# One dP tile in sixteen moved from VectorE to ScalarE and GpSimd in an attention backward

## The chip, the cores and the metric

The kernel runs on one core of one Trainium2 chip. The metric is the device time of one execution in microseconds: 2561.26 us, the median of three runs (2560.2 to 2564.32). A core has five engines that matter here: PE (TensorE, matrix products into PSUM), DVE (VectorE), ACT (ScalarE), POOL (GpSimd) and SP (SyncE, which issues DMAs). Each runs its own queue in order, and they wait for one another by semaphores.

## The reference, cut to what matters

The kernel computes the output of one transformer block and the gradients of all its inputs, for 2048 tokens, width 512, 32 heads of 16 and a feed-forward width of 1792.

```python
def _A_ref(x, wqkv, wo):
    H = 32
    Dh = D // H
    qkv = (lambda x, *d: x.transpose(*d))((x @ wqkv).reshape(B, S, 3, H, Dh), 2, 0, 3, 1, 4)
    q, k, v = (qkv[0], qkv[1], qkv[2])
    scale = Dh ** (-0.5)
    scores = jnp.einsum('bhqd,bhkd->bhqk', q, k) * scale
    p = _softmax(scores, axis=-1)
    o = jnp.einsum('bhqk,bhkd->bhqd', p, v)
    return (lambda x, *d: x.transpose(*d))(o, 0, 2, 1, 3).reshape(B, S, D) @ wo
...
h = _layernorm(x, axis=-1) * (1 + ca) + sa
x = x + ga * _A_ref(h, A_wqkv, A_wo)
h = _layernorm(x, axis=-1) * (1 + cb) + sb
x = x + gb * _B_ref(h, B_w1, B_b1, B_w2, B_b2)
...
_out, _vjp = jax.vjp(_f, A_x, A_wqkv, A_wo, B_w1, B_b1, B_w2, B_b2, c, w_mod)
_grads = _vjp(grad_out)
```

What matters here is the gradient through the softmax. With S the scores, P = exp(S) (its normalization is folded into the operands beforehand), and dO the gradient of the heads' output, the kernel forms dP = dO V^T minus a row term (two extra rows of the operand carry it), dS = P * dP, and then dQ = dS K, dK = dS^T Q, dV = P^T dO. P and dS are never kept: they are made tile by tile from Q, K, V and dO.

## The kernel before

The forward pass takes the first 1130 us or so, with the feed-forward part and its gradients around it. Then comes `attn_bwd`, the stage that the change touches, and after it `phase6`, the gradients of the projections.

**Loops.** `attn_bwd` runs over `g` (8 sets of four heads), `jp` (2 pairs of heads in a set), `c` (4 column blocks of 512 keys), `ib0` (4 groups of `G` = 4 row blocks) and `i` (a row block of 128 queries). One (g, jp, c, ib) is a *unit*; it has two tiles of 128x512, one for each head `a` of the pair. There are 1024 units, 256 groups, 2048 tiles.

**One iteration `i`** (lines 1546 to 1569) does, for its own unit, two score matmuls (L1555, into one of three PSUM buffers `st`) and two exps on ScalarE (L1559, into `pu`, bf16, six buffers). Between a score matmul and its exp stands `dP(last, a)` for the unit *before*: a matmul into one of three PSUM buffers `dp` (L1494) and a VectorE multiply by `pu` into `ds` (L1496). The score matmul uses one half of PE's rows and the dP matmul the other, so the two run side by side. After the pair `dS(last)` puts the unit on the list `pend`; at the group's last unit it issues, on SP, the crossbar DMA transpose of the group's dS (L1504) into `dsT`.

**The lists.** At odd `i` `kv_two` takes the two oldest units of `pend` and accumulates dK and dV on PE (L1448, eight matmuls for the two units, reading `ds` and `pu`). At `i` = 3 these two are the last unit of the group before and unit 0 of the present one. At even `i` two units of `pendq` give dQ on PE (L1470, 16 matmuls of 128x16 for the two units, reading `dsT`); by then their transpose was issued nearly two groups earlier, and the group that it belongs to is three back.

**The transposes.** A group's dS is 32 blocks of 128x128 (four units, two heads, four blocks). `turn_ds`, called at `i` = 2, turns the first four (unit 0, head 0) on PE through a PSUM buffer `st` (L1513), and ScalarE copies them into `dsT[:, 0:4]` (L1514). The DMA transpose turns the other 28.

**Order.** PE, SP and GpSimd follow the order in which the program was written; VectorE and ScalarE are ordered by the framework and in the trace they follow it too. GpSimd's queue in this stage holds, once for each load, a tiny copy `tick` (L1543) that reads one element of the group before's dS, so that loads keep pace with the stage, and the load's issue (L1544). The loads are for the next pair or set of heads.

**Buffers.** `ds` has three buffers, one for each group, `dsT` four. `self.junk6` is a 128x512 f32 tile used for results that nobody reads in `phase6`; `self.csq` is one of the same size for column sums after this stage.

Of the kernel before, what the change touches and what calls it, by code (L numbers as in the profile page):

```python
# [12 lines left out]
ALU = mybir.AluOpType  # L13
# [6 lines left out]
P = 128  # L20
# [85 lines left out]
class K:  # L106
# [1315 lines left out]
    def attn_bwd(self):  # L1422
# [7 lines left out]
        tc, nc = self.tc, self.nc  # L1430
        S, D, H, NQ, ST, SC = self.S, self.D, self.H, self.NQ, self.ST, self.SC
        G = 4
# [20 lines left out]
        def turn(g, jp, kvT, s0):  # L1453

            h0 = 4 * g + 2 * jp
            n = ST // 2
            tp = stp.tile([P, n, P], BF16, name="st")
            for st in range(n):
                nc.tensor.transpose(tp[:, st, :], kvT[:, (s0 + st) * P:(s0 + st + 1) * P], self.ident[:])
            v = tp[:].rearrange("p s (t a e) -> p t s a e", t=2, a=2)  # L1460
            for t, dst in enumerate((self.dk_t, self.dv_t)):
                d = dst[:, s0:s0 + n, h0 * DH:(h0 + 2) * DH].rearrange("p s (a d) -> p s a d", a=2)
                nc.scalar.copy(d, v[:, t, :, :, 0:DH])

        def dq(u, heads):
            (T, g, jp, c, ib, i, dsT) = u
            for a in heads:
                col = (2 * jp + a) * DH
                for sub in range(4):
                    nc.tensor.matmul(accq[:, ib, a, :], lhsT=dsT[:, (i * 2 + a) * 4 + sub, :],  # L1470
                                     rhs=T["K"][:, 4 * c + sub, col:col + DH],
                                     start=(c == 0 and ib == 0 and a == 0 and sub == 0), stop=False,
                                     skip_group_check=True)
            if c == SC - 1 and ib == ST - 1 and 1 in heads:
                h0 = 4 * g + 2 * jp
                d = self.dq_t[:, :, h0 * DH:(h0 + 2) * DH].rearrange("p s (a d) -> p s a d", a=2)
                nc.vector.tensor_scalar(d, accq[:], self.scale, None, ALU.mult)

        def kv_two(n=2):
            for u in pend[2 - n:2]:  # L1480
                kv(u)
            (T, g, jp, c, ib, kvT, pu, ds) = pend[1]
            del pend[:2]
            if c % 2 and ib == ST - 1 and (g, jp) == (NQ - 1, 1):
                turnq.append((g, jp, kvT, 4 * (c - 1)))
            elif c == SC - 1 and ib == ST - 1:
                turnq.extend((g, jp, kvT, s0) for s0 in (0, ST // 2))

        def dP(u, a):

            (T, g, jp, c, ib, kvT, pu, dsg, i, grp) = u
            rd = slice(64 - 64 * jp, 128 - 64 * jp)
            dp = dpp.tile([P, 512], F32, name="dp")
            nc.tensor.matmul(dp[:], lhsT=T["dOT"][rd, ib * P:(ib + 1) * P],  # L1494
                             rhs=masked["VT"][2 * jp + a][rd, 512 * c:512 * (c + 1)], start=True, stop=True)
            nc.vector.tensor_tensor(dsg[:, i, a], dp[:], pu[:, a, :], ALU.mult)  # L1496

        def dS(u):

            (T, g, jp, c, ib, kvT, pu, dsg, i, grp) = u  # L1500
            pend.append((T, g, jp, c, ib, kvT, pu, dsg[:, i]))
            if i == G - 1:
                dsT = grp[0]
                nc.sync.dma_start_transpose(dsT[:, 4:, :], dsg[:].rearrange("p i a k -> p (i a k)")[:, 512:])  # L1504
                for i in range(G):
                    pendq.append((T, g, jp, c, ib - G + 1 + i, i, dsT))

        def turn_ds(dsg, grp):

            dsT = dtp.tile([P, 8 * G, P], BF16, name="dsT")  # L1510
            tp = stp.tile([P, 4, P], BF16, name="st")
            for b in range(4):
                nc.tensor.transpose(tp[:, b, :], dsg[:, 0, 0, b * P:(b + 1) * P], self.ident[:])  # L1513
            nc.scalar.copy(dsT[:, 0:4, :], tp[:])  # L1514
            grp.append(dsT)

        tick = self.tick
        T = self.T0
        turnq, last = [], None
        for g in range(NQ):  # L1520
            for jp in range(2):
                if jp == 0:
                    if g + 1 < NQ:
                        Tn, later = self.load_group(g + 1)
                    else:
                        Tn, later = None, self.wq_pieces(1) + self.load_wmt()
                    cut = len(later) // 2 if Tn else len(later)
                    pieces = self.pair_pieces(g, 1) + later[:cut]
                    later = later[cut:]
                elif g + 1 < NQ:  # L1530
                    pieces = self.pair_pieces(g + 1, 0) + later
                else:
                    pieces = [(self.xhat1_6[:, st, :], self.xhat1_d.rearrange("(st p) d -> p st d", p=P)[:, st, :])
                              for st in range(ST)]
                kvT = kvp.tile([P, S], BF16, name="kvT")
                total = len(pieces)
                for c in range(SC):
                    c0 = 512 * c
                    for ib0 in range(0, ST, G):
                        m = c * (ST // G) + ib0 // G  # L1540
                        while pieces and (total - len(pieces)) * SC * ST <= m * G * total:
                            if last:
                                nc.gpsimd.tensor_copy(tick[:], last[7][0:1, 0, 0, 0:1])  # L1543
                            nc.gpsimd.dma_start(*pieces.pop(0))  # L1544
                        dsg, grp = self.dsp.tile([P, G, 2, 512], BF16, name="ds"), []
                        for i in range(G):
                            ib = ib0 + i
                            q = slice(ib * P, (ib + 1) * P)
                            if turnq and i == 2:
                                turn(*turnq.pop(0))  # L1550
                            pu = self.pup.tile([P, 2, 512], BF16, name="pu")
                            for a in range(2):
                                stt = stp.tile([P, 512], F32, name="st")
                                rs = slice(64 * jp, 64 * jp + 64)
                                nc.tensor.matmul(stt[:], lhsT=T["QT"][rs, q], rhs=masked["KT"][2 * jp + a][rs, c0:c0 + 512],  # L1555
                                                 start=True, stop=True)
                                if last:
                                    dP(last, a)
                                nc.scalar.activation(pu[:, a, :], stt[:], ACT.Exp, scale=self.scale)  # L1559
                            if last:  # L1560
                                dS(last)
                            last = (T, g, jp, c, ib, kvT, pu, dsg, i, grp)
                            if i % 2 == 1 and len(pend) >= 4:
                                kv_two()
                            elif i % 2 == 0 and len(pendq) > 2 * G:
                                for _ in range(4 if len(pendq) > 3 * G else 2):
                                    dq(pendq.pop(0), [0, 1])
                            if i == 2:
                                turn_ds(dsg, grp)
            T = Tn  # L1570
        with tc.manual_schedule(engines=ALL):
            for t in (2, 0):
# [338 lines left out]
```

The softmax here doesn't subtract the row's maximum and nothing guards it: scores larger than these inputs give would overflow.

## Time and profile before

| what | value |
|---|---|
| median of the runs | 2561.26 us (2561.26, 2564.32, 2560.2) |
| span of the profiled execution, first to last instruction | 2562.0 us |
| granted PE clock, mean over the span | 0.994 |
| PE busy over the span | 2483.2 us (97%) |
| ScalarE busy | 2314.2 us (90%) |
| VectorE busy | 1767.4 us (69%) |
| GpSimd busy | 569.5 us (22%) |
| first and last DMA transpose of dS (L1504) | 1185.6 and 2440.0 us |
| from one group to the next, undisturbed | 4.78 us |

The profile is of one execution; its own time is not listed apart from its span. The span lies inside the spread of the runs. Lines of the profile name the source line, the engine, the operation, and `out<-in` by the program's tile names; a figure in the last column is idle time of the engine before such instructions, with what ended it. In a row of the timeline instructions of one kind that follow one another are merged (`x21`), with the start of the first and the length from there to the end of the last. Matmuls overlap: the length of one says less than the distance between starts.

### The profile page before, as it was taken

What the parts mean: (1) busy time and instruction counts of PE and PEld (TensorE: products, weight loads), DVE (VectorE), ACT (ScalarE), POOL (GpSimd) and SP (SyncE); (2) the same over time, 40 slices, a digit from 0 to 9 for tenths busy, and PEclk for the clock granted to TensorE, in tenths of its full rate; (3) what the DMA queues carried; (4) which work ended last, traced back from release to release, by engine and by line L of the source; (5) the groups of instructions that cost most, each with busy time, mean ns of one, the idle gap of its engine ahead of it and who ended that gap; (6) DMA issues with size and microseconds to landing.
All of it is one profiled execution on the core that took longest, in us unless ns stands there. A gap on an engine that the chain in (4) does not pass through costs nothing.

```text
span 2562.0 us, 77852 instructions
## 1 busy us (share of the span) xinstructions
PE 2483.2 (97%) x31239; PEld 1227.4 (48%) x31239; DVE 1767.4 (69%) x3651; ACT 2314.2 (90%) x3757; POOL 569.5 (22%) x1137
## 2 busy tenths in 40 slices
PE   8999899999999999899999999999999999999998
PEld 4555555555555554663444444444444444444443
DVE  6222323323322344667999999999999999999957
ACT  7999999999999996436999999999999999999935
POOL 3554521320221131353011111111111111111223
PEclk9999999999999999999999999999999999999999
DMA  4588742450351153799999999999999999999997
GB/s 165 118 180 196 173 95 83 100 113 22 112 128 49 39 143 113 154 190 211 205 205 202 199 200 201 203 204 200 197 199 198 208 201 197 201 201 229 213 202 191
DMA packets 1193040, 425.37 MB, mean 166 GB/s; under 512 B 1138004, under 2 KB 1161686, under 8 KB 1192678
## 3 DMA queue, kind: packets, MB, share of 16 engines
q1 hardware_dynamic: 1153542, 319.25, 64.2%
q0 software_dynamic: 37056, 100.11, 13.1%
q8 instruction: 244, 4.00, 0.6%
q10 hardware_dynamic: 2080, 1.05, 0.1%
q14 instruction: 118, 0.97, 0.1%
HBM read 73.73 MB, written 62.40 MB: 53 GB/s over the span
## 4 chain that ended last, share of the span: by engine, by line
PE 67%; ACT 20%; DMA 5%; issue 4%; POOL 2%; DVE 1%; SPq 1%; POOLq 0%; DVEq 0%; ACTq 0%
PE st L1555 20%; ACT pu L391 16%; PE acckv L1448 11%; PE accq L1470 8%; PE st L388 7%; PE accbank L322 3%; PE dp L1494 3%; ACT pu L1559 2%; PE st L1513 2%; PE dps L1047 2%; PE pps L1234 2%; PE dp L1604 1%; PE st L1699 1%; DMA dsT<-ds 1%; DMA ev_tm<-ev_fm 1%
## 5 line engine op out<-in xcount | busy, mean ns | idle before, releaser
L1496 DVE TENSOR_TENSOR ds<-dp,pu 128x512 bf16<-128x512 f32 x2048 | 1236.2, 679 | 13.1 <-PE dp L1494 10.2
L1559 ACT ACTIVATE pu<-st 128x512 bf16<-128x512 f32 x2048 | 1073.7, 612 | 46.4 <-PE dp L1494 22.5
L391 ACT ACTIVATE pu<-st 128x1024 bf16<-128x1024 f32 x992 | 912.1, 1077 | 4.6 <-PE st L388 4.4
L388 PE MATMUL st<-QTm,KTq 128*128 128x512 bf16 x1984 | 588.6, 377 | 19.5 <-ACT pu L391 6.0
L322 PEld LDWEIGHTS <-pu 128*128 128x128 bf16 x8192 | 347.5, 96 | 236.1 <-issue 3.1
L322 PE MATMUL accbank<-Vaug,pu 128*128 128x17 bf16 x8192 | 357.7, 171 | 1.2 <-ACT Vaug L522 0.9
L1494 PE MATMUL dp<-m,q 64*128 64x512 bf16 x1024 | 345.7, 382 | 1.1 <-DVE g2w L1053 0.7
L1494 PE MATMUL dp<-m,dOTg 64*128 64x512 bf16 x1024 | 344.6, 381 | 0.1
L1470 PEld LDWEIGHTS <-dsT 128*128 128x128 bf16 x8192 | 239.5, 96 | 213.8 <-issue 209.7
L1555 PE MATMUL st<-m,q 64*128 64x512 bf16 x1024 | 319.5, 382 | 9.2 <-ACT pu L1559 7.5
L1555 PE MATMUL st<-m,QTg 64*128 64x512 bf16 x1024 | 318.9, 381 | 9.5 <-ACT pu L1559 7.8
L388 PEld LDWEIGHTS <-KTq 128*128 128x128 bf16 x1984 | 188.3, 96 | 176.9 <-issue 125.5
L1543 POOL COPY tick<-ds 1x1 bf16<-1x1 bf16 x223 | 39.6, 178 | 1005.4 <-DVE ds L1496 1005.4
L1448 PE MATMUL acckv<-ds,q 128*16 128x512 bf16 x1024 | 154.0, 381 | 0.0
L1448 PE MATMUL acckv<-pu,dOg 128*16 128x512 bf16 x1024 | 154.0, 381 | 0.0
L1448 PE MATMUL acckv<-ds,Qg 128*16 128x512 bf16 x1024 | 154.0, 381 | 0.0
L1448 PE MATMUL acckv<-pu,q 128*16 128x512 bf16 x1024 | 154.0, 381 | 0.0
L1514 ACT COPY dsT<-st 128x512 bf16<-128x512 bf16 x256 | 152.4, 595 | 1.0 <-PE st L1513 1.0
L1470 PE MATMUL accq<-Kg,dsT 128*128 128x16 bf16 x4096 | 143.3, 170 | 3.4 <-DMA dsT<-ds 3.4
L1470 PE MATMUL accq<-q,dsT 128*128 128x16 bf16 x4096 | 143.6, 170 | 0.4 <-DMA dsT<-ds 0.3
L302 POOL DMA_DIRECT2D QTm<-QTq_d x124 | 63.3, 512 | 341.3 <-PE st L388 320.2
L329 DVE RECIPROCAL rl<-accbank 128x4 f32<-128x4 f32 x128 | 22.9, 179 | 162.6 <-PE accbank L322 162.5
(379 smaller groups left out, 2864.8 us busy)
## 6 DMA issues: line engine op xcount, KB each, us to landing
KTq<-KTq_d POOLq DMA_DIRECT2D x24, 512.0 KB, 3.9
duT_d<-auT POOLq DMA_DIRECT2D x3, 1792.0 KB, 7.8
aT_d<-rT POOLq DMA_DIRECT2D x3, 1792.0 KB, 11.1
KTq_d<-KTq SPq DMA_DIRECT2D x32, 128.0 KB, 2.0
QTq_d<-ev_fm SPq DMA_DIRECT2D x32, 128.0 KB, 3.9
VTq_d<-vT POOLq DMA_DIRECT2D x4, 1024.0 KB, 6.8
dsT<-ds SPq DMA_TRANSPOSE x256, 6.7
dx<-dx_d SPq DMA_DIRECT2D x16, 256.0 KB, 4.4
```

Source lines behind the costliest of these rows:

```text
L302: nc.gpsimd.dma_start(QTm[j][32 * j:32 * j + 32, :], self.QTq_d[g, 32 * j:32 * j + 32, 512 * qc:512 * (qc + 1)])
L322: nc.tensor.matmul(acc[:, a, sub, :], lhsT=pu[:, a, sub * P:(sub + 1) * P], rhs=Vaug[:, kb, h, :], start=(kb == 0 and a == 0 and sub == 0) ...
L388: nc.tensor.matmul(stt[:, a, :], lhsT=KT[:, kb * P:(kb + 1) * P], rhs=QTm[2 * jp + a][:], start=True, stop=True)
L391: nc.scalar.activation(pu[:], stt[:], ACT.Exp, scale=self.scale)
L1047: nc.tensor.matmul(pt[:], lhsT=a[st], rhs=g_tm[:, st, :], start=(st == 0), stop=(st == ST - 1))
L1448: nc.tensor.matmul(acckv[r:r + DH, :], lhsT=T[n][:, ib, col:col + DH], rhs=src[:, a, :], start=(ib == 0), stop=(ib == ST - 1))
L1470: nc.tensor.matmul(accq[:, ib, a, :], lhsT=dsT[:, (i * 2 + a) * 4 + sub, :], rhs=T["K"][:, 4 * c + sub, col:col + DH], start=(c == 0 and i ...
L1494: nc.tensor.matmul(dp[:], lhsT=T["dOT"][rd, ib * P:(ib + 1) * P], rhs=masked["VT"][2 * jp + a][rd, 512 * c:512 * (c + 1)], start=True, sto ...
L1496: nc.vector.tensor_tensor(dsg[:, i, a], dp[:], pu[:, a, :], ALU.mult)
L1514: nc.scalar.copy(dsT[:, 0:4, :], tp[:])
L1555: nc.tensor.matmul(stt[:], lhsT=T["QT"][rs, q], rhs=masked["KT"][2 * jp + a][rs, c0:c0 + 512], start=True, stop=True)
L1559: nc.scalar.activation(pu[:, a, :], stt[:], ACT.Exp, scale=self.scale)
```

## The change

In every second group (`off(c, ib)`: the second and fourth of the four groups of a column block), one of the eight dP tiles, unit 0 and head 1, isn't multiplied by VectorE. `dP` returns the PSUM tile instead; after the exp that follows, ScalarE copies it to one of two f32 scratch tiles (`junk6` and `csq` in turn) and GpSimd multiplies the copy by P into the same place of `ds`. In the same groups `turn_ds` takes a `dsT` buffer but does no PE transposes and no ScalarE copy, and the DMA transpose turns all 32 blocks.

```diff
             nc.tensor.matmul(dp[:], lhsT=T["dOT"][rd, ib * P:(ib + 1) * P],
                              rhs=masked["VT"][2 * jp + a][rd, 512 * c:512 * (c + 1)], start=True, stop=True)
+            if a == 1 and i == 0 and off(c, ib):
+                return dp
             nc.vector.tensor_tensor(dsg[:, i, a], dp[:], pu[:, a, :], ALU.mult)
+
+        def off(c, ib):
+            return (c * SC + ib // G) % 2 == 1
+
+        def dP_pool(u, dp):
+            (T, g, jp, c, ib, kvT, pu, dsg, i, grp) = u
+            f = (self.junk6, self.csq)[(c * SC + ib // G) // 2 % 2]
+            nc.scalar.copy(f[:], dp[:])
+            nc.gpsimd.tensor_tensor(dsg[:, i, 1], f[:], pu[:, 1, :], ALU.mult)
...
             if i == G - 1:
-                dsT = grp[0]
-                nc.sync.dma_start_transpose(dsT[:, 4:, :], dsg[:].rearrange("p i a k -> p (i a k)")[:, 512:])
+                dsT, n = grp
+                nc.sync.dma_start_transpose(dsT[:, n:, :], dsg[:].rearrange("p i a k -> p (i a k)")[:, n * P:])
...
-        def turn_ds(dsg, grp):
+        def turn_ds(dsg, grp, skip):
 
             dsT = dtp.tile([P, 8 * G, P], BF16, name="dsT")
+            grp.extend((dsT, 0 if skip else 4))
+            if skip:
+                return
             tp = stp.tile([P, 4, P], BF16, name="st")
             for b in range(4):
                 nc.tensor.transpose(tp[:, b, :], dsg[:, 0, 0, b * P:(b + 1) * P], self.ident[:])
             nc.scalar.copy(dsT[:, 0:4, :], tp[:])
-            grp.append(dsT)
...
-                                if last:
-                                    dP(last, a)
+                                held = dP(last, a) if last else None
                                 nc.scalar.activation(pu[:, a, :], stt[:], ACT.Exp, scale=self.scale)
+                                if held is not None:
+                                    dP_pool(last, held)
...
                             if i == 2:
-                                turn_ds(dsg, grp)
+                                turn_ds(dsg, grp, off(c, ib))
```

## The prediction

> **What bounds the kernel now.** The change touches only the backward attention stage (about 1179 to 2443 us), so I read the page for the engines, then windows of the stage, the timeline of one group of four units, the chain, and last the landings of the crossbar transposes. A group is one pass of the `ib0` loop: four units, eight dP tiles, one transpose of dS by SP. There are 256. I write (u,a) for the tile of unit u of a group and head a.
>
> From the page, then two windows of 4.78 us, one group each (columns: engine busy us and count, PE clock, DMA share, GB/s):
>
> ```profile
> PE 2483.2 (97%) x31239; PEld 1227.4 (48%) x31239; DVE 1767.4 (69%) x3651; ACT 2314.2 (90%) x3757; POOL 569.5 (22%) x1137
> ...
> L1496 DVE TENSOR_TENSOR ds<-dp,pu 128x512 bf16<-128x512 f32 x2048 | 1236.2, 679 | 13.1 <-PE dp L1494 10.2
> ...
> L1514 ACT COPY dsT<-st 128x512 bf16<-128x512 bf16 x256 | 152.4, 595 | 1.0 <-PE st L1513 1.0
> ...
> 1697.00:1701.78 4.78, 4.78 (x77) 2.08 (x74) 4.78 (x9) 4.77 (x11) 0.63 (x3) 1.00 0.90 208
> 1701.78:1706.57 4.78, 4.78 (x73) 2.00 (x71) 4.78 (x9) 4.63 (x10) 0.69 (x3) 1.00 1.00 209
> ```
>
> PE, VectorE and ScalarE all look full, at full clock, and GpSimd is idle. Which one sets the pace is decided by who waits. VectorE's row has 13 us of idle time in 1236. The timeline (start, length, engine, line):
>
> ```profile
> 1699.69 12.63 DVE L1496 TENSOR_TENSOR ds<-dp,pu 128x512 bf16<-128x512 f32 x21
> 1702.64 3.07 ACT L1559 ACTIVATE pu<-st 128x512 bf16<-128x512 f32 x6
> 1705.87 1.08 ACT L1559 ACTIVATE pu<-st 128x512 bf16<-128x512 f32 x2 [0.16 <-PE dp L1494]
> 1706.94 0.59 ACT L1514 COPY dsT<-st 128x512 bf16<-128x512 bf16 x1
> ...
> 1704.81 0.17 PE dp L1494
> 1706.05 0.12 PE dp L1494
> ```
>
> Twenty-one VectorE multiplies without a gap take 12.63 us, so one starts every (12.63 - 0.68)/20 = 0.598 us, and eight are 4.78 us, exactly the group's period (the PE transposes start at 1701.74, 1706.52, 1711.31). The last two lines are of the chain: PE's second dP matmul of a pair starts late, by 0.17, 0.12 and (at 1703.73) 0.05 us, because its PSUM buffer, one of three, is still with VectorE. So VectorE is the bound; PE could do a group in 4.78 - 0.34 = 4.44 us. ScalarE starts an activation every (3.07 - 0.61)/5 = 0.49 us; nine are 4.4 us.
>
> **The change, part by part.** It acts in every second group ("odd", 128 of them).
>
> VectorE loses one multiply in an odd group: at most 0.598 us, over 128 groups 76.5 us. That is the ceiling of the gain.
>
> PE loses four transposes in an odd group: the chain has them as "PE st L1513 x4", 0.24 us. PE could do an odd group in 4.20.
>
> ScalarE loses the copy of the transposed block (595 ns) and gains a copy of 128x512 f32 out of PSUM; the same form elsewhere takes 572 to 598 (L1762, L1071, L1621). Net nothing. But it sits elsewhere: after the second exp of the iteration i=1, where the trace starts the next exp at 1705.87. The exps of i=2 come 0.2 us later (1706.07); the VectorE multiply that needs the first starts at about 1707.1, and it is ready at 1706.66, so 0.4 us cover this. The copy waits for a dP matmul that is over at 1704.98, long before its turn.
>
> GpSimd gains 128 multiplies of 128x512. None of this mixed form is in the trace; the nearest are L1147 (bf16 by f32 into bf16) at 1163 ns and L1054 (all f32) at 1283. I take L1147, whose types are the same in the other order, and keep 1.28 as the other end. GpSimd's own queue: a tick and a load issue stand behind the multiply and go from 1705.88 to about 1707.5; the loads are for a later pass of 16 groups, which covers 1.6 us. Would it slow VectorE? Where L1054 ran at 1180.28 for 1.28 us, three ds multiplies beside it took
>
> ```profile
> 1180.28 1.28 POOL L1054 TENSOR_TENSOR dgb_acc<-dgb_acc,g2w 128x512 f32<-128x512 f32 x1
> 1180.61 1.89 DVE L1496 TENSOR_TENSOR ds<-dp,pu 128x512 bf16<-128x512 f32 x3
> ```
>
> which is (1.89 - 0.68)/2 = 0.605 apart: no more than 0.01 us. Zero, then. In contrast the VectorE cast L1158 has a median of 424 ns and a longest of 1379, among GpSimd's L1112. The Trainium skill ("SBUF — State Buffer", on who interferes with whom) says that GpSimd and some VectorE instructions lock each other out of a shared port for a whole instruction, but not one with a single SBUF input in a one-port mode, as ds has; were the lock to hold here, 128 x 1.2 us would be lost and the sum would be some +77 us.
>
> Now the order. I follow one odd group with the trace's times for what comes before. VectorE starts dS tile (0,0) at 1705.07 and could start (1,0), now next in line, at 1705.67; but that dP matmul starts on PE at 1705.45, after the kv matmuls, and ends at 1705.83, so VectorE starts at 1705.90: 0.23 us of the 0.598 are lost to PE's order. Then it runs (1,1) at 1706.50, (2,0) at 1707.10, (2,1) at 1707.70, and is free for (3,0) at 1708.30.
>
> PE meanwhile has the one new wait. The second kv unit of iteration i=3 reads the GpSimd tile. In the trace its matmuls start at 1707.59; without the transposes at 1707.35. The ScalarE copy starts at 1705.60 (0.48 after the exp at 1705.13) and ends at 1706.19. GpSimd starts 0.13 later (what the tick takes after its VectorE write, 1705.75 to 1705.88), ends at 1706.32 + 1.16 = 1707.48, and PE goes on at about 1707.56: a stall of 0.21, which eats most of the 0.24 of the transposes. Queued behind it: 0.32 of kv, then the pair with dP (3,0), over 0.385 later, and VectorE 0.075 after: 1707.56 + 0.78 = 1708.34 against 1708.30. So 0.04 more lost; with 1.28 us on GpSimd, 0.16. VectorE's gain per odd group is 0.598 - 0.23 - 0.04 = 0.33 us (0.21 at the slow end; 0.37 with no stall). In the even group after it PE starts 0.33 behind its old lead and has its 0.34 of buffer waits to make that up, so VectorE stays the bound there. 128 x 0.33 = 42 us.
>
> The Trainium skill ("GPSIMD Engine Reference", Engine selection) advises against elementwise work on GpSimd, two-input operations being about 2x slower than on VectorE. The rows give 1163 against 679, 1.7x; an estimate by the page, 2 x 0.68 = 1.36 us, would stall VectorE by 0.24 and leave 0.13 us, 16 us in all.
>
> SP turns 32 blocks instead of 28 in odd groups.
>
> ```profile
> L1504 SPq DMA_TRANSPOSE dsT<-ds x225: 3370/3623/4895, 1297.8 to 2398.5; - x113
> DMA to landing us min/median/max: 5.1/6.5/8.1
> 1695.55 3.64 SPq L1504 DMA_TRANSPOSE dsT<-ds  x1
> 1703.71 0.56 PE L1470 MATMUL accq<-Kg,dsT 128*128 128x16 bf16 x16
> ```
>
> Issue takes SP 3.62 us for 28 blocks, so 4.14 for 32, within the 4.45 to 4.78 between issues, and landing moves by about 0.52. dq reads a group's dsT 8.16 us after its issue (1695.55 to 1703.71: it runs three groups behind). Pairing all issues with landings and dq, the spare time is 1.8 us in the median, below 0.67 in a tenth. It shrinks by 0.33 for all and by 0.85 for odd groups: about a fifth of these then wait some 0.4 us, 128 x 0.2 x 0.4 = 10 us. Half of it falls into PE's spare time in even groups; with the even groups' own few waits I charge 6 (0 to 13). SP's transpose now waits for GpSimd too, which is done 2 us before VectorE's last tile; nothing but the next transpose stands behind it.
>
> Before the stage and after 2443 us nothing changes, save that PE waits 10.9 us at the very end for a transpose that shares the DMA engines with loads; the shifted loads may move that by 3 us either way. Zero.
>
> The scratch tiles `junk6` and `csq` come back after four groups (18 us) and cost no wait.
>
> Sum: -42 + 6 = -36. The profiled span is 2562.0 us and the median of the runs 2561.26, 0.03% apart, so the sum can be made against either: 2561.3 - 36 = 2525.
>
> **The rivals.** *Nearly the whole 76 us*: PE's lead suffices after all, 2561 - 76 = 2485. For it: VectorE is the bound by the plainest reading. Against: the 0.23 us at (1,0) follow from PE's written order.
>
> *GpSimd comes late*: the operation takes 1.4 us or its start is later, and PE stands at kv. With 1.4 us the gain is 0.09 us a group less part of the crossbar's 6 us: about -10, 2551. For it: the mixed form is not in the trace and the margin is negative already.
>
> *No change*: PE, 97% busy and 67% of the chain, is the true bound. 2561. Against: the buffer waits in the chain, and PE loses transposes too.
>
> *Slower, by the crossbar*: DMA is 90 to 100% busy in the windows, and the loads that wait behind GpSimd now run together with transposes. dq then waits for dsT. If odd landings take L, PE stands L - 7.83 less 0.34 of its own spare, and every stretch x of a pair of groups gives 0.85x back (8.16 of the pair's 9.57 us): x = (L - 8.17)/1.85. With L = 9.0 (the longest 8.1 plus 0.52, and 0.4 for loads), x = 0.45, which outweighs 0.33: 128 x 0.12 = 15, 2576. It decides from L about 8.8; I expect 7.0.
>
> **How the numbers follow.** Forecast 0.58 (own range 2514 to 2547: 0.37 us and no crossbar wait; 0.21 us and 13 us of it); nearly all 0.08; GpSimd late 0.14; no change 0.06; crossbar 0.14. The measurement tells apart about 0.2%, 5 us. Faster: 0.58 + 0.08 + 0.12 of the late case = 0.78; same 0.06 + 0.02 = 0.08; slower 0.14. The range 2500 to 2562 leaves out the crossbar and most of the near-full case, 0.2.
>
> **What would show it.** In the profile after: L1496's successor at x1920 with some 0.26 us of VectorE idle per odd group put down to PE dp; odd groups near 4.45 us and even ones at 4.78; a GpSimd multiply of about 1.16 us that starts 0.13 us after the copy; a short wait of PE at acckv for GpSimd. Wrong would be: ds multiplies above 0.69 us (a port), a GpSimd operation over 1.3 us, or waits at accq for dsT of more than 10 us in all.

## The result and the profile after

The changed kernel takes 2544.02 us (median of four runs, 2538.75 to 2545.66) against 2560.73 for the kernel before on the same chip; the ratio is 0.9937, with a 95% interval of 0.9922 to 0.9951. It is 16.7 us faster, where 36 were forecast.

From the page of the changed kernel: engines, and then the groups of the stage (line, engine, operation, busy us and mean ns, idle time before and what ended it). The row after them is the kernel before's for the last one.

```profile
PE 2453.8 (96%) x30727; PEld 1201.3 (47%) x30727; DVE 1700.3 (67%) x3523; ACT 2299.9 (90%) x3757; POOL 707.1 (28%) x1265
...
L1498 DVE TENSOR_TENSOR ds<-dp,pu 128x512 bf16<-128x512 f32 x1920 | 1169.9, 681 | 67.9 <-PE dp L1494 46.6
...
L1507 POOL TENSOR_TENSOR ds<-junk,pu 128x512 bf16<-128x512 f32 x64 | 74.1, 1157 | 412.6 <-ACT junk L1506 412.6
...
L1470 PE MATMUL accq<-Kg,dsT 128*128 128x16 bf16 x4096 | 143.7, 170 | 10.3 <-DMA dsT<-ds 9.9
```

```profile
L1470 PE MATMUL accq<-Kg,dsT 128*128 128x16 bf16 x4096 | 143.3, 170 | 3.4 <-DMA dsT<-ds 3.4
```

VectorE's row is 66 us shorter (1236.2 to 1169.9), but its idle time rose from 13 to 68 us: it is no longer the engine that sets the pace everywhere. GpSimd's multiply is what it was taken for, 1157 ns, and the multiplies of VectorE beside it still take 681. In the last row PE's idle time at dQ, waiting for the crossbar, has grown from 3.4 to 9.9 us.

The time from one group's transpose to the next (SP's issue; a group has the interval that ends with its own), by place of the group in its column block. These are medians; the first three groups of a head pair, where `turn` transposes the finished pair's dK and dV, are left out. The changed groups are the second and the fourth:

| kernel | first | second | third | fourth | four |
|---|---|---|---|---|---|
| before | 4.78 | 4.84 | 4.78 | 4.78 | 19.18 |
| changed | 4.75 | 4.86 | 4.75 | 4.54 | 18.90 |

The fourth group has gained 0.24 us, the second nothing. That is where half of the forecast went. The chain of waits in a second group of the changed kernel says why (start, length, engine, tile, line):

```profile
1506.35 0.32 PE st L1568
1506.67 0.05 PE dp L1494
1506.71 0.04 issue
1506.75 0.19 ACT kvT L1451
1506.94 0.38 issue
1507.32 1.14 ACT pu L1571 x3
1508.46 0.30 issue
1508.76 0.66 ACT pu L1571
1509.41 0.11 ACT junk L1506
1509.52 0.18 issue
1509.70 0.70 ACT pu L1571
```

For three and a half microseconds the chain runs through ScalarE alone, and it starts with `kvT`, the evacuation of `acckv`: its copy out of PSUM, once a column block (702 ns, next activation 0.57 us after its start). The timeline of ScalarE over the same stretch has no gap:

```profile
1505.79 1.09 ACT L1571 ACTIVATE pu<-st 128x512 bf16<-128x512 f32 x2
1506.75 0.70 ACT L1451 ACTIVATE kvT<-acckv,kvs 128x512 bf16<-128x512 f32 x1
1507.32 2.09 ACT L1571 ACTIVATE pu<-st 128x512 bf16<-128x512 f32 x4
1509.23 0.66 ACT L1506 COPY junk<-dp 128x512 f32<-128x512 f32 x1
1509.70 1.67 ACT L1571 ACTIVATE pu<-st 128x512 bf16<-128x512 f32 x3
```

Packed, an activation of 512 columns starts every 0.478 us (four in 2.09 us: from 1507.32 to the copy at 1509.23 is 1.91). Nine of them and the evacuation are 9 x 0.478 + 0.57 = 4.87 us: the 4.86 of the second group. In ScalarE's queue the evacuation stands between the first group's last exp and the second group's first. By the clock it starts 1.6 us before the second interval of the table begins (SP issues the first group's transpose at 1508.32), because the multiplies and the transpose that end a group come that long after its last exps. VectorE feels it afterwards: in the same stretch it stands idle from 1508.89 to 1509.38, waiting for a dP matmul. In the kernel before the evacuation is at the same place of the chain:

```profile
1713.17 0.18 ACT kvT L1451
1713.36 0.39 issue
1713.74 0.63 ACT pu L1559
```

Its second group, at 4.84, was 0.06 us longer than the others; run e8 shows that this too is ScalarE's.

As for the fourth group: the VectorE timeline has the gap that the prediction worked out, after tile (0,0):

```profile
1497.73 1.88 DVE L1498 TENSOR_TENSOR ds<-dp,pu 128x512 bf16<-128x512 f32 x3
1499.83 1.29 DVE L1498 TENSOR_TENSOR ds<-dp,pu 128x512 bf16<-128x512 f32 x2 [0.23 <-PE dp L1494]
```

The engine is idle for 0.23 us, and the next multiply could have started 0.08 before the last one's end, so 0.31 of 0.598 us are lost. Over the whole stage, first to last score matmul, the profiled executions took 1256.2 us before and 1244.7 after.

### The profile page after: what moved, and what is told of

Same layout as the page of the kernel before. It is cut to its first block, busy times and chain, and to the rows that moved or that the text cites. A ratio compares the mean times of both kernels' runs of the same rounds, so it can differ in the third digit from the quotient of the medians.

```text
span 2543.9 us, 76653 instructions
## 1 busy us (share of the span) xinstructions
PE 2453.8 (96%) x30727; PEld 1201.3 (47%) x30727; DVE 1700.3 (67%) x3523; ACT 2299.9 (90%) x3757; POOL 707.1 (28%) x1265
## 4 chain that ended last, share of the span: by engine, by line
PE 58%; ACT 26%; DMA 8%; issue 5%; DVE 2%; POOL 1%; SPq 0%; DVEq 0%; ACTq 0%; POOLq 0%
ACT pu L391 18%; PE st L1568 15%; PE st L388 8%; PE acckv L1448 8%; PE accq L1470 7%; DMA dsT<-ds 7%; ACT pu L1571 6%; PE accbank L322 3%; PE dp L1494 2%; PE dps L1047 2%; PE pps L1234 2%; PE dp L1618 1%; PE pps L631 1%; PE dps L992 1%; PE st L1713 1%
## 5 line engine op out<-in xcount | busy, mean ns | idle before, releaser
L1498 DVE TENSOR_TENSOR ds<-dp,pu 128x512 bf16<-128x512 f32 x1920 | 1169.9, 681 | 67.9 <-PE dp L1494 46.6
L1507 POOL TENSOR_TENSOR ds<-junk,pu 128x512 bf16<-128x512 f32 x64 | 74.1, 1157 | 412.6 <-ACT junk L1506 412.6
L1507 POOL TENSOR_TENSOR ds<-csq,pu 128x512 bf16<-128x512 f32 x64 | 73.9, 1154 | 281.5 <-ACT csq L1506 281.5
```

The source lines that it names most:

```text
L1507: nc.gpsimd.tensor_tensor(dsg[:, i, 1], f[:], pu[:, 1, :], ALU.mult)
```

## The experiments

The theory after this reading: *ScalarE* holds the second group, because the evacuation of `acckv` falls there. Its rivals: the *crossbar* (the waits at dQ for `dsT`), and *PE's order* (every changed group is worth half).

The waits for `dsT` stand in two rows of the list of waits, PE's weight loads (`PEld`) and its matmuls (`PE`). Between 1300 and 2380 us they are 0.3 and 0.2 us in the kernel before, 20.0 and 6.4 in the changed one. The expectations below add the rows, 26 us. That counts time twice: the matmuls' waits lie inside those of the weight loads (all 6.4 us here, 19.2 of 19.4 in e1). Below, "20.0/6.4" gives both rows; the second is the time in which PE's matmuls stood still.

| run | median us | ratio to before | 95% interval |
|---|---|---|---|
| e1, third and fourth group | 2551.60 | 0.9978 | 0.9960 to 0.9997 |
| e2, fourth group only | 2546.10 | 0.9953 | 0.9937 to 0.9970 |
| e3, 28 blocks on the crossbar | 2536.45 | 0.9915 | 0.9898 to 0.9931 |
| e5, dQ an iteration later | 2539.30 | 0.9920 | 0.9893 to 0.9946 |
| e6, kernel before, dQ later | 2569.36 | 1.0054 | 1.0036 to 1.0073 |
| e7, e5 with other groups | 2541.10 | 0.9929 | 0.9899 to 0.9959 |
| e8, the crossbar part alone | 2562.29 | 1.0011 | 0.9993 to 1.0030 |
| e9, short evacuation | 2530.41 | 0.9906 | 0.9875 to 0.9937 |
| e10, third group 8 blocks on PE | 2562.05 | 1.0015 | 1.0003 to 1.0027 |
| e11, evacuation shared out | 2561.49 | 1.0002 | 0.9987 to 1.0016 |
| e12, e11 with dQ later | 2548.97 | 0.9960 | 0.9947 to 0.9973 |

Run e4 is the kernel before once more, for its trace. The runs are from several chips, each beside the kernel before on its own chip (2557.65 to 2559.02 us there), so the ratios are what can be compared, with the changed kernel's 0.9937 (0.9922 to 0.9951). The times of a group below are medians as in the table above.

**e1: the changed groups moved away from the evacuation.**

```diff
-            return (c * SC + ib // G) % 2 == 1
+            return ib // G >= 2
-            f = (self.junk6, self.csq)[(c * SC + ib // G) // 2 % 2]
+            f = (self.junk6, self.csq)[ib // G % 2]
```

> The changed groups are the third and fourth of each column block instead of the second and fourth. Theory ScalarE: the second group gains nothing because the evacuation of acckv (L1451, 0.57 us) falls into it, and with nine other activations at 0.478 us ScalarE needs 4.87 us there; the third has no such evacuation. Then the third and fourth groups take about 4.5 us each, the second goes back to 4.84, four groups take 18.6 us instead of 18.9: 64 x 0.28 = 18 us faster than the changed kernel, about 2526. Rival crossbar: two transposes of 32 blocks now follow each other, PE's waits at accq for dsT in the stage grow from 26 us to 45 or more, and the time is 2540 to 2550. Rival PE order: every changed group gives the same half of the expected gain wherever it lies, 2544.

The groups did what the ScalarE theory said: 4.75, 4.84, 4.54, 4.57, 18.70 in all. The time did what the crossbar rival said, and a little worse than its 2540 to 2550. PE's waits, from the list of waits between 1300 and 2380 us (us in total, times, longest), first in the changed kernel, then in e1:

```profile
PEld L1470 <- DMA dsT<-ds: 20.0, 38, 1.8
...
PE accq L1470 <- DMA dsT<-ds: 6.4, 13, 1.4
```

```profile
PEld L1470 <- DMA dsT<-ds: 34.4, 48, 2.5
PE accq L1470 <- DMA dsT<-ds: 19.4, 32, 2.4
```

They went from 20.0/6.4 to 34.4/19.4 us: two sets of 32 blocks in a row are too much at the faster pace, and the mean of four groups, late landings included, is 19.18 us against 19.13 in the changed kernel. The first column block of each head pair lost too: its second to fourth groups read 5.61, 5.69, 4.91 against 5.43, 5.62, 4.54, 0.62 us in 16 cases. Added up over the trace, these groups of the first column blocks take 256.8 us against 248.5, and the twelve groups of a head pair after them 918.2 against 917.3. So behind the first column blocks the late landings ate what the groups gained, and the 8 us by which the stage is longer lie in the first column blocks, whose cause was not tested.

**e2: only the fourth group.** The first line of the diff above becomes `return ib // G == 3`.

> Only the fourth group of each column block is changed, 64 groups instead of 128. Theory ScalarE: the second group's change was worth nothing, so this one is as fast as the changed kernel or up to 6 us faster (fewer blocks on the crossbar), 2538 to 2544. Rival, each changed group gives alike: half of the 16.7 us is lost, 2552. Rival crossbar as the main loss: half the extra blocks, waits at accq for dsT below 12 us in the stage, about 2536.

Groups of 4.75, 4.84, 4.78, 4.54: 18.91, against 18.90 with twice as many changed groups. The change in the second group was worth nothing undisturbed. The waits for `dsT` fell to 6.5/2.9 us. The stage takes 1245.9 us against 1244.7. The time, 0.9953 against 0.9937, is not told apart from the changed kernel's; but half of the gain, 0.9968, lies inside its interval too, so it is the groups and the stage that speak against the rival, not the time.

**e3: the crossbar's four extra blocks taken away.** A part of dQ is left out.

```diff
-            grp.extend((dsT, 0 if skip else 4))
+            grp.extend((dsT, 4))
             if skip:
+                nc.gpsimd.memset(dsT[:, 0:4, :], 0.0)
                 return
```

> As the changed kernel, but the DMA transpose turns 28 blocks in every group; in the changed groups the other four blocks of dsT are set to zero by GpSimd, so a part of dQ is left out. Theory crossbar: PE's waits at accq for dsT between 1300 and 2380 us fall from 26 us to below 8 (before: 0.6), the last transpose lands sooner, and the time falls by 8 to 12 us to about 2534. Theory ScalarE alone: the undisturbed groups keep 4.54 and 4.86 us, and the time stays within 3 us of 2544.

The waits (same list) are all but gone, the groups are those of the changed kernel (4.75, 4.86, 4.75, 4.54), and the ratio is 0.0022 lower, 5.6 us; the stage of the profiled execution is 6.5 us shorter (1238.2), close to the 6.4 us that the matmuls had waited. The intervals of the two ratios overlap, so the size is rough, but not what became of the waits:

```profile
PEld L1470 <- DMA dsT<-ds: 1.2, 1, 1.2
PE accq L1470 <- DMA dsT<-ds: 1.1, 1, 1.1
```

Both theories hold here at once: the crossbar costs some 6 us, and 4.86 in the second group does not come from it.

**e4: the kernel before again.**

> The kernel before once more, for a second trace. In the trace of the changed kernel the stage starts 8.8 us earlier than in that of before (first score matmul at 1169.8 against 1178.6 us), though nothing ahead of it was changed. If that is a spread between executions or chips, the first score matmul is here at some other place between 1168 and 1180; if the change moved it, it is at 1178 again. The groups of the stage should be at 4.78 us and its length (first to last score matmul) at 1256 us in either case.

The first score matmul is at 1171.4 us and the stage takes 1257.4. The 8.8 us by which the changed kernel's trace reached the stage earlier are a spread, not an effect: in the other traces here it starts at 1167 to 1176 us.

**e5 and e6: dQ an iteration later**, in the changed kernel and, as a control, in the kernel before.

```diff
-                            if i % 2 == 1 and len(pend) >= 4:
+                            if i % 2 == 0 and len(pend) >= 4:
                                 kv_two()
-                            elif i % 2 == 0 and len(pendq) > 2 * G:
+                            elif i % 2 == 1 and len(pendq) > 2 * G:
```

> The changed kernel with dQ at odd i and dK, dV at even i (the two are exchanged), so that dQ reads a group's dsT one iteration, 1.2 us, later; no work is added or left out. Theory crossbar latency: PE's waits at accq for dsT between 1300 and 2380 us fall from 26 us to below 8 and the time falls to about 2536, as with 28 blocks. Rival, the crossbar's throughput: the landings move out with the reader and the waits stay above 15 us, time 2544. Rival ScalarE alone: no effect, 2544.

> The control: the same exchange in the kernel before. It has 0.6 us of waits at accq for dsT between 1300 and 2380 us, so nothing is to be had: within 4 us of before, groups at 4.78 us. If the exchange is worth more than that by itself (ScalarE evacuates acckv an iteration earlier, which could take the 0.06 us off the group of 4.84: 64 x 0.06 = 4 us), that much of run e5 isn't the crossbar.

In e5 the waits fell to 9.4/4.7 us, 14 as the expectation adds them, between what the two crossbar theories asked for; the time, 2539.3, is not told apart from the changed kernel's. The control went wrong: the exchange makes the kernel before 0.54% slower (groups of 4.84 instead of 4.78, the second 4.95 instead of 4.84), so it is not free and e5 does not isolate the crossbar. On top of the exchange the change is worth 30 us (2569.4 to 2539.3). In the trace of e6 the cost lies at VectorE's tiles of unit 2, which start 0.642 and 0.608 us after the tile before instead of 0.598; what holds them there was not followed up.

**e7: e5 with the groups chosen by the ScalarE theory.**

```diff
-            return (c * SC + ib // G) % 2 == 1
+            m = c * SC + ib // G
+            return m in (1, 3) or (m >= 4 and m % 4 >= 2)
...
```

> The exchange of e5, and the changed groups chosen by the ScalarE theory: third and fourth of each column block, where acckv is not evacuated, but second and fourth in the first column block of a head pair, where the third group has the transposes of kvT; 128 groups as in the changed kernel. ScalarE theory with the crossbar wait gone: four groups take 18.6 us in three of four column blocks (18.9 in the changed kernel), 16 groups 76.4 us instead of 77.2: 12 us below e5, about 2524. Rival crossbar: two transposes of 32 blocks in a row bring waits at accq for dsT of over 20 us, and the time is 2535 to 2545.

A miss: 2541.1. With the exchange the evacuation comes an iteration earlier, right beside the copy of the PE transposes; an unchanged second group then takes 5.0 us and a changed one 4.71 (e5), so there is nothing to be had by moving. It also shows a limit of the theory: 4.87 us is not a floor for every group that has the evacuation. In e5 it stands in the first group's part of ScalarE's queue, yet that group takes 4.80 us and the second, without it, 4.71. Where in the queue it stands matters, and that was not worked out further. The waits for `dsT` were 7.6/4.0 us and did not decide it.

**e8: the crossbar part without the offload.**

```diff
-            if a == 1 and i == 0 and off(c, ib):
-                return dp
```

> Only the second half of the change: in the changed groups the crossbar turns all 32 blocks, PE's transposes and ScalarE's copy of them fall away, and VectorE multiplies every tile as before. Theory VectorE bound: groups stay at 4.78 us; the second group of a column block goes from 4.84 to 4.78 as ScalarE has a copy less (4 us in all); waits at accq for dsT of 5 to 15 us cost up to that: 2553 to 2562, with the kernel before at 2559. If PE were the bound, its 0.24 us in 128 groups would come off: 2528.

All four groups are at 4.78, the second too: ScalarE has a copy less there, and its 0.06 us go. PE's 0.24 us in every second group bring nothing, so PE was not the bound. The waits for `dsT` are 33.3/13.0 us in this stretch, far more than expected, and the time is not told apart from before.

**e9: the evacuation made short.** Three quarters of dK and dV are left out, and one `kvT`, set to zero once, serves all head pairs.

```diff
-                nc.scalar.activation(kvT[:, 512 * c:512 * (c + 1)], acckv[:], ACT.Copy, scale=kvs[:])
+                nc.scalar.activation(kvT[:, 512 * c:512 * c + 128], acckv[:, 0:128], ACT.Copy, scale=kvs[:])
...
+        kvT = kvp.tile([P, S], BF16, name="kvT")
+        nc.vector.memset(kvT[:], 0.0)
...
-                kvT = kvp.tile([P, S], BF16, name="kvT")
```

> The changed kernel, but ScalarE evacuates only 128 of acckv's 512 columns (the rest of kvT is set to zero once), so three quarters of dK and dV are left out. ScalarE's step of 0.57 us becomes about 0.26 (L1463 does 256 columns in 0.264). ScalarE theory: the second group of a column block is bound by ScalarE's nine activations and this one, 9 x 0.478 + 0.57 = 4.87 us measured 4.86, and goes to 4.55 us or so; 64 x 0.31 = 20 us faster than the changed kernel, about 2524, less what the faster pace adds in waits for dsT (the waits grow from 26 us). Rival, PE's order or the crossbar holds that group: it stays at 4.86 and the time at 2541 to 2544.

This is the direct test. The evacuation's row, in the changed kernel and in e9 (minimum, median and maximum ns):

```profile
L1451 ACT ACTIVATE kvT<-acckv,kvs x64: 687/702/717, 1194.4 to 2418.0; 128x512 bf16<-128x512 f32 x64
```

```profile
L1451 ACT ACTIVATE kvT<-acckv,kvs x64: 368/382/398, 1193.1 to 2407.0; 128x128 bf16<-128x128 f32 x64
```

With 0.32 us less on ScalarE, once in four groups, the second group goes from 4.86 to 4.54 us, by just that; 4.54 is also what the fourth group takes without an evacuation, so ScalarE need not be the only bound there any more. No other group got shorter. In time less arrives. The stage of the profiled execution is 8.5 us shorter (1236.2), of the 20; the ratio falls by 0.0031, 8 us, with intervals that overlap (one of the four runs took 2543.67). The waits for `dsT` rise to 29.3/13.3 us, which is about half of what is missing; the rest was not found.

**e10: PE takes four more blocks in the third group**, with one ScalarE copy of 1024 columns: `turn_ds` gets the number of blocks, 8 where `ib // G == 2`.

> The changed kernel, and in the third group of each column block PE turns eight blocks instead of four, with one ScalarE copy of 1024 columns: 116 blocks in four groups for the crossbar instead of 120 (before: 112). Crossbar theory: the waits at accq for dsT fall from 26 us to 10 to 15 us and the time to 2539 to 2542, if the copy (some 0.4 us longer) finds room beside VectorE's 4.78 us in that group: ScalarE needs 8 x 0.478 + 0.9 = 4.72. If it doesn't, the third group goes from 4.75 to above 4.9 us and the time to 2546 to 2555.

The waits for `dsT` fell to 5.6/3.8 us, but ScalarE had no room: the wide copy takes 1020 ns where the narrow one takes 588, the third group goes to 4.89 and the fourth to 4.80, and the gain is gone.

**e11 and e12: the evacuation shared between ScalarE and VectorE**, without and with e5's exchange.

```diff
-                nc.scalar.activation(kvT[:, 512 * c:512 * (c + 1)], acckv[:], ACT.Copy, scale=kvs[:])
+                nc.scalar.activation(kvT[:, 512 * c:512 * c + 256], acckv[:, 0:256], ACT.Copy, scale=kvs[:])
+                nc.vector.tensor_scalar(kvT[:, 512 * c + 256:512 * (c + 1)], acckv[:, 256:512], kvs[:], None, ALU.mult)
```

> The changed kernel with the evacuation of acckv shared out: ScalarE takes 256 columns, VectorE the other 256; nothing is left out. ScalarE theory: in the second group ScalarE needs 9 x 0.478 + 0.31 = 4.61 us and VectorE 7 x 0.598 + 0.35 = 4.54, so the group goes from 4.86 to about 4.6, 64 x 0.26 = 17 us less before the crossbar's part; in run e9 12 of 20 us arrived, so 8 to 12 us faster than the changed kernel, 2532 to 2536. Rival: the VectorE half falls into the group before, whose eight multiplies already fill it, and that group goes from 4.75 to 5.05; then nothing is gained, 2540 to 2546.

> As e11, and dQ exchanged with dK, dV as in e5. There the second group was at 4.71 already. If the waits for dsT are what eats e11's gain, this is faster than e11: 2528 to 2534. If the exchange's own cost (even groups of 4.80 instead of 4.75, 128 x 0.05 = 6 us) outweighs it: as e5 or slower, 2537 to 2542.

The rivals were right in kind, and too mild: e11 is at 2561 where nothing gained meant 2540 to 2546, so the whole gain is gone, and e12 is slower than e5. VectorE's half falls into the first group, whose eight multiplies fill it already, and that group goes from 4.75 to 5.18 us (5.14 in e12, from 4.80). In e12 the second group is then at 4.54, in e11 still at 4.85; there PE's list of waits has 17 us at `dp` for the ScalarE copy, which the changed kernel does not have; so the 4.61 that the ScalarE sum gave was missed there for another reason. No version here is told apart from the changed kernel on the better side with its whole work done.

## Why the prediction was half right

*VectorE is the bound, and taking one of its tiles away is the gain.* Right, in three of the four groups of a column block (e8: with PE relieved and VectorE not, 4.78 everywhere).

*"ScalarE loses the copy of the transposed block and gains a copy... Net nothing."* This is the step that failed, and behind it the count "nine are 4.4 us". The count of nine leaves out the evacuation of `acckv`, which comes once in four groups. Net nothing was true, but the engine already stood at 4.87 us in the second group, where VectorE was to be brought down to 4.45. There the term of 0.33 us is 0 (4.84 before, 4.86 after): 64 of the 128 groups, 21 of the 42 us. e9 shows it from one side, the groups of e1, e2 and e8 from others. The lines were in the chain of before; I had read one group of a kind that has no evacuation.

*0.23 us lost to PE's order.* The place was right and the idle time is 0.23 us to the hundredth, but counted from start to start 0.31 are lost: VectorE began 0.14 us after the matmul's end, not 0.075. The fourth group gained 0.24 us and the first and third 0.035 each, together 0.31 against 0.33: this half of the forecast came.

*The new wait of PE at dK, dV for GpSimd.* Wrong, and without effect. I had `pend` one unit too short: five units are on it when two are taken, so unit 0 of a group is used at `i` = 1 of the next group, not at `i` = 3 of its own (so the description of `kv_two` ahead of the prediction is an iteration pair too early). No list of waits has PE at `acckv` waiting for GpSimd. The price of GpSimd itself was right: 1157 and 1154 ns against 1163.

*The crossbar, 6 us.* Right in mechanism and about in size: SP's issue of 32 blocks takes 4.15 us (4.14 forecast), the median landing moves from 6.6 to 7.1 us, and taking the blocks away is worth 6.5 us of the stage (e3). The matmuls' waits are 6.4 us in the stretch counted here and 13.5 over the whole stage, above the 10 us that the prediction named as a sign of being wrong; in the kernel before they are 3.7 over the stage. This place also makes further gains small: in e1 and e9 the matmuls wait another 13 and 7 us there.

*The sum.* By the table, four groups are 0.29 us shorter, 64 x 0.29 = 18.5 us, less 6.5 at the crossbar is 12. That is what the stage lost in the profiled executions: 11.5 us, or 12.7 against e4's trace. By medians 16.7 were measured, with 12.5 to 20 as the interval of the ratio; the 4 or 5 us between are not explained, and may be chance.

## What to carry to other kernels

When several engines are within a few per cent of one another, do the sum for every kind of period, those with the rare instruction too, not for one typical period: relieving the engine that bounds most of them is worth nothing in those that another one holds. A rare line in the chain of waits (0.19 us of `kvT`) is the sign of such a period. And the latency of a transfer that runs ahead by a fixed number of steps has to be compared with those steps at the new pace, since each gain shortens the lead.

## What the runs showed of the hardware that was not expected

The latency of the crossbar has a spread, and its late end decides. With 28 blocks a group a transpose landed 6.6 us after issue in the median (5.7 to 7.6 for the middle eight tenths), with 30 on average 7.1 (6.1 to 8.2). From landing to the first dQ matmul the median fell from 1.84 to 1.09 us and the shortest tenth from below 0.66 to below 0.05. So half a microsecond more, at a slightly faster pace, took the matmuls' waits from 0.2 to 6.4 us, and with two sets of 32 blocks in a row they were 19.4. And exchanging two blocks of PE work (e6), with no work added, cost the kernel before 11 us (0.54% by the ratio).
